# Running dV up to eight heads ahead of dK in the backward part of a decode-attention kernel

## The chip, the cores and the metric

The kernel runs on one core of one Trainium2 chip. A core has five engines with a stream of instructions each: TensorE (PE, matmuls), VectorE (DVE), ScalarE (ACT), GpSimd (POOL) and SyncE (SP). SyncE only waits and issues transfers between the chip's main memory and the on-chip memory; the transfers are carried out by 16 DMA engines. The metric is the time of one execution on the device, in microseconds (us). Before the change it is 1714.82 us, the median of three runs (1712.49 to 1715.11).

## The reference

What is computed is the forward pass of one transformer block for one new token in each of four sequences, with the attention against a cache, and then the gradients of eight of its inputs, the two caches among them:

```python
def _A_ref(x, k_cache, v_cache, wq, wo):       # B=4, Sq=1, D=512; H=32, Sk=4096, Dh=128
    q = (x @ wq).reshape(B, Sq, H, Dh).transpose(0, 2, 1, 3)
    scores = einsum("bhqd,bhkd->bhqk", q, k_cache) * Dh ** -0.5
    p = softmax(scores)
    o = einsum("bhqk,bhkd->bhqd", p, v_cache)
    return o.transpose(0, 2, 1, 3).reshape(B, Sq, H * Dh) @ wo
h  = x + _A_ref(layernorm(x), k_cache, v_cache, wq, wo)
h2 = h + swiglu(layernorm(h), w1, w3, w2)      # F=1792
# outputs: h2, and the gradients of x, k_cache, v_cache, wq, wo, w1, w3, w2 for a given grad_out
```

There are 4 x 32 = 128 pairs of sequence and head; the kernel calls each pair a head and numbers them s = 0 to 127. The K and the V of a head are 4096 x 128 numbers in bf16 each, 1024 KB. For a single query the gradients of the caches are outer products. With dO the gradient of the head's output o:

- dV = p (4096 numbers) times dO (128 numbers): it needs p and dO, and no cache.
- dP = V dO, and from it dS = p (dP - c) times the scale, with c = the sum of o dO.
- dK = dS (4096 numbers) times q (128 numbers): it needs dP, and so V once more.

## The kernel before

The program order of each engine is the order in which the code below calls its instructions. The forward part reads every K and V once. The backward part, which the change touches, reads every V a second time and writes 128 dV and 128 dK of 1024 KB each.

**Slots.** All large tiles live in 23 slots of on-chip memory. A slot that is given back is appended to a queue and taken again from its front; whoever takes it waits until the work that still uses it is over. In the backward part seven slots make up a ring of their own for V. At the beginning four are left for the outputs dV and dK; more come free later.

```python
def outer(dst, col2, row):                     # one VectorE multiply of 128 x 4096
    nc.vector.tensor_tensor(out=dst..., in0=col2..., in1=row..., op=ALU.mult)

def grad_V(s):
    gv = Slot("gv")
    outer(gv.heads(), P2s.pop(s), reps["rdo", s // REP][:, s % REP, :])
    nc.sync.dma_start(out=rows_of(out_3[b, h]), in_=gv.heads())
    if s > 1: gv.give()
    else:     first_gv.append(gv)              # dV(0) and dV(1): given back later

def grad_K(s):
    gk = Slot("gk")
    outer(gk.heads(), dS2s[s // B][:, s % B], reps["rq", s // REP][:, s % REP, :])
    nc.sync.dma_start(out=rows_of(out_2[b, h]), in_=gk.heads())
    gk.give()
```

`outer` needs the row (dO or q of the head) on all 128 partitions. `replicate` makes this for a group of REP = 4 heads: four matmuls against columns of the identity, and a ScalarE copy into one of two buffers in turn. `P_pairs` is a GpSimd copy that lays out p for `outer`, in three buffers in turn.

```python
def replicate(i0):
    for nm_, rows in (("rdo", dOrows_bf), ("rq", qrows_bf)):
        if (nm_, i0 // REP) in reps: continue
        ps = psrep.tile([P, REP, Dh], FP32, tag="rep", name="rep_ps")
        for i in range(REP): nc.tensor.matmul(ps[:, i, :], lhsT=ident_b[...], rhs=rows[0:K_, :], ...)
        rt = rep_bufs[nm_][i0 // REP % 2]
        nc.scalar.copy(out=rt, in_=ps[:])
        reps[nm_, i0 // REP] = rt
```

**The front of a head** makes its row of dP. V lies with the 4096 keys on the partitions and has to be transposed first:

```python
def front(s):
    for g in range(4):                         # V_T: 8 PE transposes, one ScalarE copy back over V
        V_T(s, psT, range(g, g + 1))
        if s % 4 == 0 and g == 0: rows_out()   # the last group's four rows of dP: PSUM to SBUF
        if s % 4 == 0 and g == 2: rows_T()     # ... and transposed on PE
    dO_window(s + 2)                           # GpSimd: the dO column for a later front
    # 8 matmuls: dP of the head into rows of one PSUM tile
    # the slot of V(s) goes to the ring (or to the outputs, when the ring has its seven)

def group_dS(g): ...                           # VectorE: dS of four heads, from the transposed dP
```

**The loop.** `load_ahead` issues a load of V for each slot in the ring. All transfers below are issued by SyncE, in this order: one whose data or slot isn't ready holds up those behind it. At most eight are in flight, as each waits for the eighth before it.

```python
# dV(0), dV(1) have been issued in the stage before
O0, S0, L, LV = 2, 21, 5, 3
for s in range(L):
    load_ahead(s); P_pairs(s); front(s)
    if s < 2:        first_gv[s].give()
    elif s < LV + 1: grad_V(s)
group_dS(0)
for s in range(NH):
    load_ahead(s + L)
    if s % REP == 0 and s + REP < NH: replicate(s + REP)
    P_pairs(s + L)
    if s + L < NH: front(s + L)
    elif s + L == NH: rows_out(); rows_T()
    if s > 0 and s + LV < NH: grad_V(s + LV)
    grad_K(s)
    if s % B == B - 1 and s + 1 < NH: group_dS((s + 1) // B)
    if s >= S0: step("s", 3 if s < S0 + 15 else 2)   # pieces of the weight gradients and of dx
    elif s >= O0: step("o")                          # pieces of dO for the later heads
```

Of the kernel before, what the change touches and what calls it, by code (L numbers as in the profile page):

```python
# [9 lines left out]
FP32 = mybir.dt.float32  # L10
# [14 lines left out]
def kernel(  # L25
# [22 lines left out]
    nc = tc.nc  # L48
    P = nc.NUM_PARTITIONS
# [5 lines left out]
    Dh = A_k_cache.shape[3]  # L55
    F = B_w1.shape[1]
    NH = B * H
# [105 lines left out]
    ident_b = const.tile([P, P], BF16, name="ident_b")  # L163
# [14 lines left out]
    def ones_window(col):  # L178
# [11 lines left out]
                          in_=rowg[:, None, :, None].to_broadcast([P, 4, 8, 4]))  # L190
# [70 lines left out]
    with ExitStack() as c0:  # L261
# [11 lines left out]
        for h in range(H):  # L273
            for cc in range(DC):
                nc.tensor.matmul(qT_ps[:, h, :], lhsT=wq_s[cc].b(HD)[:, h * Dh:(h + 1) * Dh], rhs=xhatT[:, cc, :],
                                 start=(cc == 0), stop=(cc == DC - 1))
# [4 lines left out]
        for r in range(2):  # L281
            for t_ in range(2):
                for q in range(4):
                    nc.tensor.matmul(qr_ps[32 * q:32 * (q + 1), 2 * r + t_, :], lhsT=ident_b[:, 64 * r + t_:64 * (r + 1):2],
                                     rhs=qT_bf[:], start=True, stop=True, tile_position=(0, 32 * q))
# [314 lines left out]
    def step(k, n=1):  # L600
        for _ in range(n):
            next(units[k], None)
# [114 lines left out]
    dOrows_bf = pers2.tile([NH, Dh], BF16, name="dOrows_bf")  # L717
# [4 lines left out]
    qrows_bf = pers2.tile([NH, Dh], BF16, name="qrows_bf")  # L722
# [29 lines left out]
    REP = B  # L752
    reps = {}
# [13 lines left out]
    P2s, first_gv = {}, []  # L767

    def outer(dst, col2, row):
        nc.vector.tensor_tensor(  # L770
            out=dst.rearrange("p j (r t) -> p j r t", t=2),
            in0=col2[:, :, None, :].to_broadcast([P, SJ, Dh // 2, 2]),
            in1=row.rearrange("p (r t) -> p r t", t=2)[:, None, :, :].to_broadcast([P, SJ, Dh // 2, 2]),
            op=ALU.mult,
        )

    def grad_V(s):
        b, h = bh_of(s)
# [3 lines that stand above are left out]
        if s > 1:  # L782
            gv.give()
        else:
            first_gv.append(gv)
# [14 lines left out]
    with ExitStack() as cm:  # L800
# [33 lines left out]
        for wi, wt in enumerate((w1, w3)):  # L834
            for fc in range(FC):
                for cc in range(DC):
                    nc.tensor.matmul(gu_ps[:, wi, fc, :], lhsT=w13_view(wt, cc)[:, fc * P:(fc + 1) * P], rhs=hhatT[:, cc, :],
                                     start=(cc == 0), stop=(cc == DC - 1))
# [25 lines left out]
        for jj in range(DC):  # L864
            i_mm = 0
            for (lt, wt) in ((d_gateT_bf, w1), (d_upT_bf, w3)):
                for fc in range(FC):
                    nc.tensor.matmul(dn_ps[:, jj, :], lhsT=w13_view(wt, jj)[:, fc * P:(fc + 1) * P], rhs=lt[:, fc, :],
                                     start=(i_mm == 0), stop=(i_mm == 2 * FC - 1))
                    i_mm += 1  # L870
        for sl in w1 + w3:
            sl.give()
        rs = Slot("reps")
        rep_bufs = {nm_: [rs.b()[:, (2 * k + i) * 512:(2 * k + i + 1) * 512].rearrange("p (i d) -> p i d", i=REP) for i in range(2)]
                    for k, nm_ in enumerate(("rq", "rdo"))}
# [4 lines left out]
        ps = psA.tile([P, REP, Dh], FP32, tag="rT", name="repq_ps")  # L880
# [4 lines left out]
        for s in range(3):  # L885
# [8 lines left out]
                         start=True, stop=True)  # L894
# [32 lines left out]
    with ExitStack() as c2:  # L927
        psT = c2.enter_context(tc.tile_pool(name="psT2", bufs=2, space=bass.MemoryType.PSUM))
        psD = c2.enter_context(tc.tile_pool(name="psD", bufs=1, space=bass.MemoryType.PSUM))
        psrep = c2.enter_context(tc.tile_pool(name="psrep", bufs=1, space=bass.MemoryType.PSUM))  # L930
# [174 lines left out]
        def rest_of_dO():  # L1105
            for pg in range(1, H // 8):
                while wo_units and wo_units[0] < 4 * (pg + 1):
                    woT_unit(psT, wo_units.popleft(), "s")
                    yield
                dO_columns(8 * pg, 8 * pg + 8, psg, "gps")  # L1110
                yield
                dO_rows(8 * pg, 8 * pg + 8, psg, "gps")
                mid_w["wo"][pg].give()
                yield
            dr_ps = psg.tile([B, D], FP32, tag="gps", name="dr_ps")
            for c in range(DC):
                nc.tensor.transpose(dr_ps[:, c * P:(c + 1) * P], dhT_f[:, c, :], ident_f[:])
            nc.scalar.copy(out=dh, in_=dr_ps[:])

        units["o"] = rest_of_dO()  # L1120
        def replicate(i0):
            K_ = 8 * B if i0 < 8 * B else P
            for nm_, rows in (("rdo", dOrows_bf), ("rq", qrows_bf)):
                if (nm_, i0 // REP) in reps:
                    continue
                ps = psrep.tile([P, REP, Dh], FP32, tag="rep", name="rep_ps")
                for i in range(REP):
                    nc.tensor.matmul(ps[:, i, :], lhsT=ident_b[0:K_, i0 + i:i0 + i + 1].to_broadcast([K_, P]), rhs=rows[0:K_, :],
                                     start=True, stop=True)
                rt = rep_bufs[nm_][i0 // REP % 2]  # L1130
                nc.scalar.copy(out=rt, in_=ps[:])  # L1131
                reps[nm_, i0 // REP] = rt

        rows = {}
        dS2s = {}
# [4 lines left out]
        def dO_window(s):  # L1140
            if s < NH:
                nc.gpsimd.tensor_copy(out=zd[s % B][:, 32:132:67], in_=dOT_bf[:, s:s + 1].to_broadcast([P, 2]))  # L1142

        def P_pairs(s):
            if s < NH and s not in P2s:
                P2s[s] = bw3.tile([P, SJ, 2], BF16, tag="P2", name="P2")
                nc.gpsimd.tensor_copy(out=P2s[s][:], in_=P_all[:, s, :, None].to_broadcast([P, SJ, 2]))  # L1147

        def rows_out():
            if "ps" in rows:  # L1150
                rows["sb"] = bw3.tile([P, 512], FP32, tag="dPr", name="dPr", bufs=1)
                nc.scalar.copy(out=rows["sb"][:], in_=rows.pop("ps")[:])  # L1152

        def rows_T():
            if "sb" in rows:
                sb = rows["t"] = rows.pop("sb")
                rows["T"] = psD.tile([P, B, P], FP32, tag="dPT", name="dPT_ps")
                for jj in range(4):
                    nc.tensor.transpose(rows["T"][:, jj, :], sb[:, jj * P:(jj + 1) * P], ident_f[:])  # L1159
# [46 lines left out]
                load_V2(nc.sync)  # L1206


        O0, S0, L, LV = 2, 21, 5, 3

        def load_ahead(s):
            prefetch()
            if s < NH and s not in V2s and s not in VTs:
                load_V2(nc.sync)

        for s in range(2):
            dO_window(s)
        for s in range(L):
            load_ahead(s)
            P_pairs(s)  # L1220
            front(s)
            if s < 2:
                first_gv[s].give()
            elif s < LV + 1:
                grad_V(s)
        group_dS(0)
        for s in range(NH):
            load_ahead(s + L)
            if s % REP == 0 and s + REP < NH:
                replicate(s + REP)  # L1230
            P_pairs(s + L)
            if s + L < NH:
                front(s + L)
            elif s + L == NH:
                rows_out()
                rows_T()
            if s > 0 and s + LV < NH:
                grad_V(s + LV)
            grad_K(s)
            if s % B == B - 1 and s + 1 < NH:  # L1240
                group_dS((s + 1) // B)
            if s >= S0:
                step("s", 3 if s < S0 + 15 else 2)
            elif s >= O0:
                step("o")
# [31 lines left out]
```

## Time and profile before

The profile is of one execution of 1712.58 us, with a span of 1710.6 us from its first to its last instruction.

| | busy us | share of the span |
|---|---|---|
| PE matmuls | 1253.6 | 73% |
| PE weight loads | 928.1 | 54% |
| VectorE | 1236.0 | 72% |
| ScalarE | 968.4 | 57% |
| GpSimd | 410.8 | 24% |
| transfers | 707.50 MB | mean 414 GB/s |

The shares are averages over stages: the forward part takes about the first 660 us, a short middle stage (the second layernorm, the MLP, its gradients, dO) follows to about 700 us, and the rest is the backward loop. The rows of slices cut the span into 40 equal parts of 42.8 us, and each digit is a share in tenths. In a timeline, a row has its start, its duration, the engine, the line of the kernel, the operation, what it writes and reads, and, in brackets, for how long the engine was idle before it and what ended that. L781 is the issue of a dV, L1201 that of a dK, L797 that of a load of V; `gv` and `gk` are the tiles of dV and dK. The multiplies behind dV and dK (L770) take 2.3 us each on VectorE.

### The profile page before, as it was taken

The page shows a single profiled execution, that of the slowest core. Times are in us where ns is not written, and L with a number is a line of the kernel's source. Part 1 is how long each engine was busy: PE and PEld are TensorE (multiplying, and loading weights), DVE is VectorE, ACT ScalarE, POOL GpSimd, SP SyncE. Part 2 cuts the span into 40 slices and gives each one's busy share as a digit, 9 for nine tenths or more (in the row PEclk, how much of TensorE's full clock was granted, in tenths as well). Part 3 has the DMA queues.
Part 4 walks back from the last instruction along what each step waited for, and adds up shares of the span by engine and source line. Part 5 has one row for each costly group of instructions (what it writes and reads, how often), then busy time and mean ns, then how long its engine had stood idle before and what let it go on. Part 6 is the DMA issues. An engine that isn't in the chain of part 4 may idle for free. (4 is left out here: it accounts for less than half of the span.)

```text
span 1710.6 us, 38404 instructions
## 1 busy us (share of the span) xinstructions
PE 1253.6 (73%) x16180; PEld 928.1 (54%) x16180; DVE 1236.0 (72%) x1294; ACT 968.4 (57%) x1502; POOL 410.8 (24%) x680
## 2 busy tenths in 40 slices
PE   5889888888888888776689977766566665666650
PEld 4777766767676666644467755533344433443440
DVE  5989999999998996467677457765476566566672
ACT  3556444544544444677664468775668665675540
POOL 1211232222222321132112146420022223300220
PEclk9999999999999999899886589995889787787775
DMA  9999999999999999899999999999999999999996
GB/s 401 424 425 423 425 423 425 424 424 423 416 423 411 422 407 399 311 389 426 425 425 426 426 397 425 425 426 426 426 426 426 425 424 420 424 423 413 410 424 280
DMA packets 101741, 707.50 MB, mean 414 GB/s; under 512 B 11052, under 2 KB 15288, under 8 KB 17600
## 3 DMA queue, kind: packets, MB, share of 16 engines
q1 hardware_dynamic: 101152, 704.95, 99.0%
q8 instruction: 127, 2.08, 0.5%
q14 instruction: 46, 0.38, 0.1%
q0 software_dynamic: 416, 0.10, 0.0%
HBM read 422.59 MB, written 282.34 MB: 412 GB/s over the span
## 5 line engine op out<-in xcount | busy, mean ns | idle before, releaser
L765 ACT COPY V<-pt_tps 128x1024 bf16<-128x1024 bf16 x512 | 490.2, 1025 | 146.3 <-PE pt_tps L764 124.3
L764 PE MATMUL pt_tps<-ident_b,V 128*128 128x128 bf16 x4096 | 359.1, 249 | 206.3 <-ACT V L765 178.9
L764 PEld LDWEIGHTS <-V 128*128 128x128 bf16 x4096 | 306.7, 114 | 271.1 <-issue 231.1
L770 DVE TENSOR_TENSOR gv<-P,reps 128x4096 bf16<-128x4096 bf16 x125 | 286.9, 2295 | 162.9 <-DMA out_dram<-gv 115.5
L770 DVE TENSOR_TENSOR gk<-dS,reps 128x4096 bf16<-128x4096 bf16 x128 | 293.3, 2293 | 95.3 <-DMA out_dram<-gv 85.4
L421 DVE TENSOR_TENSOR PK<-Kn,PK 128x4096 bf16<-128x4096 bf16 x128 | 292.4, 2284 | 26.1 <-POOL PK L417 25.7
L436 PE MATMUL M_ps<-PK,Vn 128*128 128x130 bf16 x4096 | 285.2, 222 | 30.9 <-DMA Vn<-in_A_v_cache_dram 30.4
L436 PEld LDWEIGHTS <-Vn 128*128 128x128 bf16 x4096 | 253.2, 99 | 50.5 <-DMA Vn<-in_A_v_cache_dram 42.0
L1147 POOL COPY P<-P_all 128x64 bf16<-128x64 bf16 x127 | 121.5, 957 | 552.7 <-DVE gv L770 547.6
L328 DVE STREAM_TRANSPOSE KT<-Kn 128x512 f32<-128x512 f32 (+1 forms) x321 | 250.7, 797 | 0.3 <-issue 0.2
L323 ACT COPY KT<-pt_tps 128x1024 bf16<-128x1024 bf16 x128 | 129.5, 1012 | 184.9 <-PE pt_tps L322 150.1
L1177 PE MATMUL dP_ps<-V,zd 128*32 128x512 bf16 x1024 | 182.9, 439 | 66.7 <-ACT V L765 64.0
L334 POOL TENSOR_TENSOR W<-qrep,wmask 128x128 bf16<-128x128 bf16 x128 | 124.0, 969 | 82.1 <-PE S_ps L354 67.4
L417 POOL COPY PK<-P_all 128x64 bf16<-128x64 bf16 x128 | 32.6, 255 | 414.3 <-ACT P_all L411 411.3
L1142 POOL COPY zd<-dOT_bf 128x2 bf16<-128x2 bf16 x128 | 116.2, 908 | 65.7 <-PE dP_ps L1177 65.7
L1177 PEld LDWEIGHTS <-zd 128*32 128x32 bf16 x1024 | 37.6, 95 | 156.3 <-issue 141.1
L1131 ACT CAST reps<-rep_ps 128x512 bf16<-128x512 f32 x62 | 36.4, 586 | 129.4 <-DVE gk L770 97.7
L1191 DVE TENSOR_SCALAR dPr<-dPT_ps,c_rep 128x32 f32<-128x32 f32 x128 | 23.2, 242 | 89.3 <-PE dPT_ps L1159 89.2
L411 ACT COPY P_all<-pt_P 32x64 bf16<-32x64 bf16 x256 | 52.1, 204 | 53.2 <-PE pt_P L407 50.9
L322 PE MATMUL pt_tps<-ident_b,Kn 128*128 128x128 bf16 x1024 | 80.5, 223 | 0.0
L446 PE MATMUL kP_ps<-PK,onesw 128*32 128x512 bf16 x1024 | 79.2, 386 | 0.0
L386 ACT ACTIVATE E<-S_ps,nm 128x256 f32<-128x256 f32 x64 | 30.4, 475 | 82.0 <-DVE nm L383 82.0
(239 smaller groups left out, 1315.0 us busy)
## 6 DMA issues: line engine op xcount, KB each, us to landing
Kn<-in_A_k_cache_dram SPq DMA_DIRECT2D x128, 1024.0 KB, 15.3
Vn<-in_A_v_cache_dram SPq DMA_DIRECT2D x128, 1024.0 KB, 15.6
V<-in_A_v_cache_dram SPq DMA_DIRECT2D x128, 1024.0 KB, 19.8
out_dram<-gv SPq DMA_DIRECT2D x128, 1024.0 KB, 20.0
out_dram<-gk SPq DMA_DIRECT2D x128, 1024.0 KB, 20.1
wq<-in_A_wq_dram SPq DMA_DIRECT2D x8, 1024.0 KB, 15.5
out_dram<-gw SPq DMA_DIRECT2D x6, 896.0 KB, 19.7
wo<-in_A_wo_dram SPq DMA_DIRECT2D x4, 1024.0 KB, 11.7
```

The lines of the kernel that those rows point to most:

```text
L322: nc.tensor.transpose(pt[:, i, :], Kn[:, c * GW + i, :], ident_b[:])
L323: nc.scalar.copy(out=KT[:, c * GW:(c + 1) * GW, :], in_=pt[:])
L328: nc.vector.transpose(out=KT[:, c * w_:(c + n) * w_], in_=Kn[:, c * w_:(c + n) * w_])
L334: nc.gpsimd.tensor_tensor(out=W[:, hl], in0=qrep[:, :, s:s + 1].to_broadcast([P, 4, 32]), in1=wmask[:, hl, None, :].to_broadcast([P, 4, 32 ...
L421: nc.vector.tensor_tensor(out=PK[:, :, 0:Dh].rearrange("p j (r t) -> p j r t", t=2), in0=Ks[s].heads().rearrange("p j (r t) -> p j r t", t=2),
L436: nc.tensor.matmul(hold["M"][:], lhsT=Vn[:, j, :], rhs=PK[:, j, :], start=(j == 0), stop=(j == SJ - 1))
L764: nc.tensor.transpose(pt[:, i, :], v[:, g * GW + i, :], ident_b[:])
L765: nc.scalar.copy(out=v[:, g * GW:(g + 1) * GW, :], in_=pt[:])
L770: nc.vector.tensor_tensor(out=dst.rearrange("p j (r t) -> p j r t", t=2), in0=col2[:, :, None, :].to_broadcast([P, SJ, Dh // 2, 2]), in1=r ...
L1142: nc.gpsimd.tensor_copy(out=zd[s % B][:, 32:132:67], in_=dOT_bf[:, s:s + 1].to_broadcast([P, 2]))
L1147: nc.gpsimd.tensor_copy(out=P2s[s][:], in_=P_all[:, s, :, None].to_broadcast([P, SJ, 2]))
L1177: nc.tensor.matmul(rows["acc"][32 * c:32 * (c + 1), :], lhsT=zq_window(zd[hl], 2 * hl + u), rhs=VT[:, j0:j0 + 4, :], start=(hl == 0 and u ...
```

## The change

dV needs neither V nor dP, only p and the replicated dO rows, so it can be made long before the dK of its head. The old loop keeps dV three heads ahead of dK. The new one lets it run further ahead from the beginning of the backward part, up to eight heads, and lets the lead fall back to three from head 60 to head 76. Three things go with it. The slots of the first two dV are both given back after the first front, instead of after the first and the second, so that the next dV can take them sooner. The replicated rows of dO and of q are made apart, each shortly before its own user. And p of heads 3 to 5 is laid out before the first front.

The aim is that the output transfers have work while the fronts of the first heads are still to come.

```diff
-        def replicate(i0):
+        def replicate(nm_, i0):
+            if i0 >= NH or (nm_, i0 // REP) in reps:
+                return
 ...                                            (the body as before, for one kind of row)
-        O0, S0, L, LV = 2, 21, 5, 3
+        O0, S0, L = 2, 21, 5
+        gvd = {"n": 2}
+
+        def more_V(upto):
+            while gvd["n"] < min(NH, upto):
+                s = gvd["n"]
+                P_pairs(s)
+                replicate("rdo", s - s % REP)
+                grad_V(s)
+                P_pairs(s + 1)
+                P_pairs(s + 2)
+                gvd["n"] += 1
+                if s % REP == 2:
+                    replicate("rdo", s + 2)
+
+        def lead_V(s):
+            return 8 - min(5, max(0, s - 56) // 4)
 ...
+        for s in range(3, 6):
+            P_pairs(s)
         for s in range(L):
             load_ahead(s)
-            P_pairs(s)
             front(s)
-            if s < 2:
-                first_gv[s].give()
-            elif s < LV + 1:
-                grad_V(s)
+            if s == 0:
+                for gv in first_gv:
+                    gv.give()
+            more_V((4, 6, 7, 8, 9)[s])
+            if s == 0:
+                replicate("rdo", REP)
         group_dS(0)
         for s in range(NH):
             load_ahead(s + L)
-            if s % REP == 0 and s + REP < NH:
-                replicate(s + REP)
-            P_pairs(s + L)
+            if s % REP == 2:
+                replicate("rq", s + 2)
 ...
-            if s > 0 and s + LV < NH:
-                grad_V(s + LV)
+            if s > 0:
+                more_V(s + 1 + lead_V(s))
             grad_K(s)
```

More of the change, by code (lines that the diff above doesn't have):

```diff
@@ L1120 @@
         units["o"] = rest_of_dO()
-        def replicate(i0):
+        def replicate(nm_, i0):
+            if i0 >= NH or (nm_, i0 // REP) in reps:
+                return
             K_ = 8 * B if i0 < 8 * B else P
[L1123 to L1132, printed above, removed]
+            rows = dOrows_bf if nm_ == "rdo" else qrows_bf
+            ps = psrep.tile([P, REP, Dh], FP32, tag="rep", name="rep_ps")
+            for i in range(REP):
+                nc.tensor.matmul(ps[:, i, :], lhsT=ident_b[0:K_, i0 + i:i0 + i + 1].to_broadcast([K_, P]), rhs=rows[0:K_, :],
+                                 start=True, stop=True)
+            rt = rep_bufs[nm_][i0 // REP % 2]
+            nc.scalar.copy(out=rt, in_=ps[:])
+            reps[nm_, i0 // REP] = rt
         rows = {}
```

## The prediction

> **What bounds the kernel now.** I read the page first (part 2, the slices), then windows of 10 us around the one slice that falls out, then the timelines of SyncE's transfers and of VectorE there, and last the waits.
>
> ```profile
> PE   5889888888888888776689977766566665666650
> ...
> PEclk9999999999999999899886589995889787787775
> DMA  9999999999999999899999999999999999999996
> GB/s 401 424 425 423 425 423 425 424 424 423 416 423 411 422 407 399 311 389 426 425 425 426 426 397 425 425 426 426 426 426 426 425 424 420 424 423 413 410 424 280
> ```
> No compute engine is full, and the transfers run at about 425 GB/s almost everywhere. The page's 707.50 MB at 425 GB/s take 1665 us, so of a span of 1710.6 us only some 46 us are lost. The slices show where: slice 17 (684 to 727 us, 311 GB/s), slice 18 (389) and the last one (280). A change of order can win only what such holes hold. This is the beginning of the backward part, by windows (the last two columns are the DMA share and GB/s):
>
> ```profile
> 700.00:710.00 10.00, 6.79 (x59) 4.42 (x56) 7.37 (x7) 5.92 (x7) 5.59 (x13) 0.66 0.89 367
> 710.00:720.00 10.00, 6.95 (x85) 4.32 (x80) 0.00 (x0) 7.52 (x8) 0.72 (x4) 1.00 0.40 107
> 720.00:730.00 10.00, 6.87 (x84) 4.66 (x80) 6.51 (x8) 7.52 (x10) 1.98 (x4) 1.00 0.88 308
> 730.00:740.00 10.00, 7.00 (x84) 4.34 (x82) 5.96 (x3) 7.53 (x9) 3.58 (x4) 1.00 0.96 331
> 740.00:750.00 10.00, 7.23 (x80) 4.36 (x78) 5.56 (x7) 7.54 (x9) 2.38 (x2) 1.00 1.01 421
> ```
> Short of 425 by 58, 318, 117 and 94 GB/s, the four windows from 700 to 740 us lose 587 x 10 / 425 = 13.8 us. In the second, VectorE is not busy at all. Its timeline and SyncE's say why:
>
> ```profile
> 707.25 2.29 DVE L770 TENSOR_TENSOR gv<-P,reps 128x4096 bf16<-128x4096 bf16 x1
> 723.31 0.73 DVE L1191 TENSOR_SCALAR dPr<-dPT_ps,c_rep 128x32 f32<-128x32 f32 x4 [13.77 <-PE dPT_ps L1159]
> ```
> ```profile
> 700.22 7.26 SPq L781 DMA_DIRECT2D out_dram<-gv  x3
> 715.45 0.34 SPq L797 DMA_DIRECT2D V<-in_A_v_cache_dram  x1
> 715.88 0.38 SPq L781 DMA_DIRECT2D out_dram<-gv  x1
> 720.44 5.87 SPq L797 DMA_DIRECT2D V<-in_A_v_cache_dram  x2
> 726.85 0.34 SPq L1201 DMA_DIRECT2D out_dram<-gk  x1
> 732.34 0.33 SPq L797 DMA_DIRECT2D V<-in_A_v_cache_dram  x1
> ```
> After four dV, VectorE waits 13.77 us for the dP of the first group of heads. Meanwhile nothing may go out: the next load of V waits until front(2) has released a slot (715.45), and the finished fourth dV stands behind it in SyncE's order. A front takes some 5 us (PE transposes, four ScalarE copies of 1025 ns, dP matmuls) and releases one load.
>
> [...]the shortest landing of a dV in the hole is 4.3 us, and 1024 KB at 425 GB/s are 2.47 us, which leaves 1.8. So one transfer at a time does not fill the engines, and it takes two or more in flight. [...]dV work, which needs no dP, goes into the stretch that waits for fronts. [...]the P copies here take 0.23 us beside an idle VectorE and 2.34 us beside a dV.
>
> **The change part by part.** *Amount of work.* None is added or removed: the same 128 dV (2.29 us each), 128 dK, as many replications (four matmuls and one ScalarE copy of 586 ns), the same bytes. Only order and slots change.
>
> *The opening.* Slots: the outputs still take turns in the same four, and the loads in the ring of seven. In the program's order seven dV transfers now precede the first ring load; then load, dV, load, dV, load, dK. Worked from the old times: dV(0) to dV(2) are unmoved (issued 700.2, 702.8, 707.1), since dV(2) takes V(0)'s slot after front(0). dV(3) may go out at once, at 709.6. dV(4) needs dV(1)'s slot (landed by about 707), the second group of replicated rows (matmuls and copy after front(0), some 1 us, in time) and its P: VectorE 709.5 to 711.8. dV(5) takes dV(2)'s slot, landed at 707.1 + 4.3 = 711.4: done 714.1. dV(6) takes dV(3)'s: 716.4. dV(7) takes V(1)'s, free since front(1): 718.7. dV(8) takes dV(4)'s: 721.0. So from 707 on one transfer goes out every 2.3 us, against 2.47 us that each takes, and from 716 on the loads come on top. The two replications put into the opening delay fronts 2 to 4 by about 1 us, and dK(0) from 726.8 to 727.7. Then front(5) no longer has two replications ahead of it and ends at about 732, as before.
>
> *The sum.* At 733.3 us the old order has issued dV 0 to 4, dK 0 and 1 and four loads since 700. The new one has issued dV 0 to 9, the same two dK and four loads: five transfers more at the same head of the fronts and of dK. 5 x 2.47 = **12.3 us**. That fits the 13.8 us that the hole holds: about 1.5 us stay (start of the first transfers, 706 to 709).
>
> *Where it is cashed.* The lead itself does not shorten the middle: at the same time the same head is in front and dK, with five more dV away. It is spent at heads 60 to 76, where five iterations leave out a dV. In the old trace dK(60) goes out at 1191 us and dK(76) at 1316, and there
>
> ```profile
> 1190.00:1320.00 130.00, 77.78 (x780) 48.30 (x780) 80.42 (x56) 83.65 (x105) 21.66 (x35) 0.85 1.01 426
> ```
> the transfers are full and PE, VectorE and ScalarE are busy 60%, 62% and 64%. Taking 12.3 us out of 130 brings PE to 66% and ScalarE to 71%. I take the whole gain as cashed. From head 76 on the lead is three again and the end is as before: the 20 us from 1690 on, at 127 GB/s, lose 14 us in both kernels.
>
> *Replicated rows made apart.* In the old order the replicated q rows for head s+4 are made at head s, into a buffer that dK(s-1) still reads, so ScalarE, and with it the next front, waits for VectorE:
>
> ```profile
> ACT reps L1131 <- DVE gk L770: 97.7, 18, 12.5
> ```
> Now they are made at head s+2 of the group before, into a buffer last read by dK five heads back from the new ones: fronts may run two heads further ahead. Off the path mostly, as the transfers are full. It helps where PE is the slower one: from 960 to 1000 us it is busy 87% at a granted clock of 0.61, SyncE waits for fronts, and just after it the transfers sink to 364, 401 and 388 GB/s (990 to 1020), a loss of 61 + 24 + 37 = 122, or 2.9 us. A larger lead of the fronts should fill part; I count 1 us.
>
> Together 12.3 + 1.0 = 13.3 us: 1714.8 - 13.3 = **1701.5 us**.
>
> **The rivals.** (a) *The gain is given back at the fronts.* Heads 60 to 76 must pass 12 us faster; if PE, slowed by its clock, can't, part is lost. For it: granted clocks of 0.5 in some windows from 1150 on. Against it: SyncE's waits from 1110 to 1400 us are for landed transfers nearly all, for PE 2.5 us. It would give 1705 to 1712. (b) *SyncE's order turns on the new kernel.* A dV now stands ahead of the next load; if a dV is late for its slot, the load behind it is late too, and later a front. For it: four output slots only, and in the old trace from 745 to 860 us SyncE waits 36.5 us for dV and 29.3 for dK. Against it: these waits lie under full transfers. It would give about 1708 to 1718. (c) *The slack of the fronts does more than I count*, and the dip at 990 to 1020 and the 401 to 413 GB/s from 1550 to 1620 us go too: 2 to 4 us more, 1697 to 1699. Slower by 2% would need a new hole of 34 us, and faster by 2% a time of 1680.5, which is the 1665 us of bytes plus the unchanged end: there is no room.
>
> **Range and chances.** Three runs of before spread over 2.6 us. Around 1701.5 I put 1696 (rival c with all of the hole) to 1709 (half of the gain given back). Chances: faster by over 2% 0.01, within 2% 0.97, slower by over 2% 0.02.
>
> **What would show it.** Right: the windows from 710 to 740 us at 400 GB/s or more, VectorE busy from 707 to 721; dK(0) issued at 727 to 728 and dK of the same head at nearly the same time until 60; five heads' transfers caught up by head 76; a span 11 to 14 us shorter. Wrong: low GB/s that returns within 710 to 800 us, fronts that start later than before, or GB/s under 420 from 1190 to 1320, where the lead is spent.

## The result, and the profile after

The changed kernel takes 1703.23 us, the median of four runs (1702.52 to 1705.36); the kernel before took 1714.96 us beside it, also in four. The ratio is 0.9937, with a 95% interval of 0.9920 to 0.9954. The prediction was 1701.5 us in a range of 1696 to 1709. The profiled spans are 1710.6 us before and 1700.7 us after, 9.9 us apart.

The slices of the kernel after (40 of 42.5 us; each digit a share in tenths, the last row the GB/s moved):

```profile
PE   5889888888888888877689877676577666666660
...
PEclk9999999999999999899976789988787877777665
DMA  9999999999999999999999999999999999999996
GB/s 401 424 425 423 424 424 424 423 424 424 414 424 411 422 406 401 385 419 425 425 425 426 425 424 425 425 426 426 424 422 422 419 421 415 419 421 410 412 425 280
```

Two things are to be seen. Slice 17, which stood at 311 GB/s, is now at 385. And in slices 30 to 36 the rate is lower than before, 422 to 415 where it had been 426 to 420. Nobody had planned for the second.

The same stretch by windows of 10 us, and the stretch in which the lead is spent (PE, PE weight loads, VectorE, ScalarE, GpSimd busy; granted clock; DMA share; GB/s):

```profile
700.00:710.00 10.00, 6.97 (x65) 4.89 (x63) 7.96 (x8) 5.76 (x8) 3.38 (x13) 0.66 0.86 356
710.00:720.00 10.00, 6.95 (x84) 4.46 (x83) 9.58 (x5) 7.72 (x9) 7.74 (x7) 1.00 1.01 418
720.00:730.00 10.00, 7.00 (x79) 4.38 (x77) 6.66 (x8) 7.49 (x10) 4.44 (x5) 1.00 0.99 361
730.00:740.00 10.00, 7.15 (x84) 4.39 (x82) 5.09 (x4) 7.76 (x10) 1.35 (x5) 1.00 1.00 423
...
1190.00:1320.00 130.00, 87.12 (x812) 55.06 (x811) 74.41 (x58) 86.96 (x110) 24.05 (x36) 0.83 1.01 423
```

Against 425 GB/s the four windows of the hole now lack 69 + 7 + 64 + 2 = 142, or 142 x 10 / 425 = 3.3 us, where they lacked 13.8. So 10.5 us of bytes were won here. PE is as busy as it was in the second to fourth window; what changed is VectorE, from 0.00 to 9.58 us in the second. SyncE's issues (start, duration, line, what is written and read, count) and VectorE's operations show the five transfers themselves:

```profile
700.74 16.61 SPq L781 DMA_DIRECT2D out_dram<-gv  x7
717.46 0.78 SPq L797 DMA_DIRECT2D V<-in_A_v_cache_dram  x1
719.22 0.33 SPq L781 DMA_DIRECT2D out_dram<-gv  x1
721.81 0.34 SPq L797 DMA_DIRECT2D V<-in_A_v_cache_dram  x1
722.25 0.53 SPq L781 DMA_DIRECT2D out_dram<-gv  x1
727.34 0.34 SPq L797 DMA_DIRECT2D V<-in_A_v_cache_dram  x1
728.24 0.33 SPq L1201 DMA_DIRECT2D out_dram<-gk  x1
732.33 0.34 SPq L797 DMA_DIRECT2D V<-in_A_v_cache_dram  x1
732.76 0.45 SPq L781 DMA_DIRECT2D out_dram<-gv  x1
733.31 0.44 SPq L1201 DMA_DIRECT2D out_dram<-gk  x1
```
```profile
707.56 6.72 DVE L770 TENSOR_TENSOR gv<-P,reps 128x4096 bf16<-128x4096 bf16 x3
714.70 6.73 DVE L770 TENSOR_TENSOR gv<-P,reps 128x4096 bf16<-128x4096 bf16 x3 [0.42 <-POOL P L1147]
724.70 0.73 DVE L1191 TENSOR_SCALAR dPr<-dPT_ps,c_rep 128x32 f32<-128x32 f32 x4 [3.27 <-PE dPT_ps L1159]
```

Up to 733.3 us ten dV (7 + 1 + 1 + 1), two dK and four loads have been issued; before it were five dV, two dK and four loads. The last dV and dK of the old count are these:

```profile
732.76 0.38 SPq L781 DMA_DIRECT2D out_dram<-gv  x1
733.23 0.38 SPq L1201 DMA_DIRECT2D out_dram<-gk  x1
```

VectorE's wait for the first dP is 3.27 us in place of 13.77. Of what is left of the hole, nearly half lies in the first window, which lacked as much before (356 GB/s now, 367 then), and nearly half in the third, at 361 GB/s: behind the dV of 722.25 nothing is issued until the load at 727.34, which waits for a front (the loads' waits for dP are up to 4.5 us here).

Where the time went is clearest in the moments at which dK of the same head is issued (my list, from the issues of L1201):

| head of dK | before, us | after, us | difference |
|---|---|---|---|
| 0 | 726.8 | 728.2 | +1.4 |
| 32 | 963.7 | 965.7 | +2.0 |
| 48 | 1090.6 | 1092.7 | +2.1 |
| 64 | 1223.0 | 1220.1 | -2.9 |
| 80 | 1351.6 | 1341.3 | -10.2 |
| 112 | 1612.5 | 1602.5 | -10.0 |
| 127 | 1689.9 | 1680.0 | -9.9 |

The five dV taken out of heads 60 to 76 bring 12.1 us (from about +2.0 to -10.1), and hardly anything of that is lost afterwards.

### The profile page after: what moved, and what is told of

It is laid out like the page before. It is cut to its first block, busy times and chain, and to the rows that moved or that the text cites. A ratio compares the mean times of both kernels' runs of the same rounds, so it can differ in the third digit from the quotient of the medians.

```text
span 1700.7 us, 38400 instructions
## 1 busy us (share of the span) xinstructions
PE 1258.0 (74%) x16180; PEld 931.3 (55%) x16180; DVE 1236.7 (73%) x1294; ACT 967.2 (57%) x1502; POOL 397.8 (23%) x678
## 3 DMA queue, kind: packets, MB, share of 16 engines
q8 instruction: 127, 2.08, 0.5%
## 5 line engine op out<-in xcount | busy, mean ns | idle before, releaser
L770 DVE TENSOR_TENSOR gv<-P,reps 128x4096 bf16<-128x4096 bf16 x125 | 286.1, 2292 | 172.1 <-DMA out_dram<-gv 132.8
L770 DVE TENSOR_TENSOR gk<-dS,reps 128x4096 bf16<-128x4096 bf16 x128 | 293.4, 2294 | 111.1 <-DMA out_dram<-gv 77.3
L1177 PE MATMUL dP_ps<-V,zd 128*32 128x512 bf16 x1024 | 179.1, 432 | 68.6 <-ACT V L765 65.8
L1147 POOL COPY P<-P_all 128x64 bf16<-128x64 bf16 x125 | 92.4, 740 | 468.7 <-DVE gv L770 468.6
L1142 POOL COPY zd<-dOT_bf 128x2 bf16<-128x2 bf16 x128 | 130.5, 1021 | 156.3 <-PE dP_ps L1177 156.3
L322 PEld LDWEIGHTS <-Kn 128*128 128x128 bf16 x1024 | 62.0, 100 | 25.8 <-issue 25.8
L400 ACT ACTIVATE Pn<-E,rl 128x1024 bf16<-128x1024 f32 x64 | 73.7, 1152 | 3.3 <-DVE rl L397 3.2
```

Source lines behind the costliest of these rows:

```text
L322: nc.tensor.transpose(pt[:, i, :], Kn[:, c * GW + i, :], ident_b[:])
L770: nc.vector.tensor_tensor(out=dst.rearrange("p j (r t) -> p j r t", t=2), in0=col2[:, :, None, :].to_broadcast([P, SJ, Dh // 2, 2]), in1=r ...
L1177: nc.tensor.matmul(rows["acc"][32 * c:32 * (c + 1), :], lhsT=zq_window(zd[hl], 2 * hl + u), rhs=VT[:, j0:j0 + 4, :], start=(hl == 0 and u ...
```

## The experiments

Every kernel below is an edit of the changed kernel, if nothing else is said, and its time is a median; ratios are to the kernel before, timed beside it (medians 1712.88 to 1714.14 us).

### 1. The replicated rows coupled again

```diff
-            if s % REP == 2:
-                replicate("rq", s + 2)
+            if s % REP == 0:
+                replicate("rq", s + REP)
```

> The changed kernel, but the replicated q rows are made again at the first head of the group before (four heads ahead, into a buffer that the dK just before still reads); the lead of dV is kept. Theory A (one of the 16 DMA engines is behind the others and sets the time; a dip of the mean rate in which that engine has work left costs nothing): the dip of GB/s between 980 and 1020 us comes back, and the time stays within 1 us of the changed kernel's 1703.2 us. Theory B (bytes per time count, as the prediction had it): the dip costs 2 to 3 us, 1705 to 1706.

Measured: 1702.73 us, ratio 0.9934 (0.9919 to 0.9949). The time is that of the changed kernel, so making the rows apart is worth nothing. But the dip at 990 to 1020 us did not come back: the four windows from 980 on moved 423, 426, 423 and 426 GB/s. That part of the expectation failed: with the larger lead of dV the dip stays away even if the rows are coupled.

### 2. Only the rows apart, in the kernel before

```diff
-            if s % REP == 0 and s + REP < NH:
-                replicate(s + REP)
+            if s % REP == 0 and s + REP < NH:
+                replicate(s + REP, "rdo")
+            if s % REP == 2 and s + 2 < NH:
+                replicate(s + 2, "rq")
```

> The kernel before, with only the replicated rows of q made two heads later (apart from those of dO), lead three as before. Theory A: the dip at 980 to 1020 us is filled, the hole at 704 to 738 us stays, and the time stays within 1 us of before, 1715. Theory B: 1712 to 1713.

Measured: 1713.47 us, ratio 0.9996 (0.9988 to 1.0005): no difference. By windows of this kernel (columns as above):

```profile
710.00:720.00 10.00, 7.16 (x83) 4.32 (x80) 0.36 (x1) 7.49 (x9) 0.72 (x4) 0.98 0.35 120
720.00:730.00 10.00, 7.00 (x86) 4.75 (x84) 5.69 (x8) 7.72 (x10) 1.27 (x3) 1.00 0.90 315
...
990.00:1000.00 10.00, 7.17 (x87) 4.64 (x87) 10.00 (x6) 8.00 (x10) 10.00 (x8) 1.00 1.01 420
1000.00:1010.00 10.00, 6.83 (x92) 5.14 (x90) 6.61 (x6) 9.68 (x12) 6.63 (x6) 1.00 1.02 428
1010.00:1020.00 10.00, 7.91 (x110) 5.67 (x108) 9.97 (x8) 6.17 (x8) 6.95 (x4) 1.00 1.01 421
```

The hole is there as before, and the dip (364, 401 and 388 GB/s before) is gone, with a granted clock of 0.66 in the window ahead of it where before had 0.54. So in the old order the coupled rows do make the dip. And yet the time is the same. A dip in the rate that can be filled for nothing was not on the path. This asked for another explanation of what sets the end; it is taken up in experiments 8 to 12.

### 3. The lead at five heads, and 4. at eleven

```diff
 def lead_V(s):
-    return 8 - min(5, max(0, s - 56) // 4)
+    return 5 - min(2, max(0, s - 56) // 4)        # 3
+    return 11 - min(8, max(0, s - 56) // 4)       # 4
 ...
-            more_V((4, 6, 7, 8, 9)[s])
+            more_V((4, 5, 6, 6, 6)[s])            # 3
+            more_V((4, 6, 8, 10, 12)[s])          # 4
```

Kernel 4 also replicates rows of heads 32 to 63 from 64 rows in place of 128, since the later rows aren't made yet when it wants them.

> The changed kernel with a lead of five instead of eight (dV up to head 5 in the opening, the lead falls to three at heads 60 to 64). If the gain is the number of dV issued more by the same head of dK, times 2.47 us: two transfers instead of five, 4.9 us less 1 to 2 us for later fronts, 1710 to 1712. If the order of the opening alone does it (both slots given back after the first front, the fourth dV not behind a load), most of the gain is there already: 1703 to 1705.

> The changed kernel with a lead of eleven (dV up to head 11 in the opening, the lead falls to three at heads 60 to 88). Three transfers more would be 7.4 us if the hole went on, 1696. But the changed kernel's hole has only some 3 us left (356 GB/s at 700 to 710 us, 361 at 720 to 730), part of it before the first dV can go, so I expect 1701 to 1704: two or three us at most, against a dK(0) that goes out later.

Measured: lead five 1708.81 us, ratio 0.9966 (0.9955 to 0.9978), 5.1 us sooner than before. That is the two transfers by which its lead exceeds the old one, 2 x 2.47 = 4.9. The hole stays half open:

```profile
710.00:720.00 10.00, 6.99 (x80) 4.33 (x80) 3.91 (x2) 7.49 (x9) 4.46 (x5) 1.00 1.01 393
720.00:730.00 10.00, 7.40 (x84) 4.75 (x84) 6.25 (x8) 7.49 (x10) 3.29 (x3) 1.00 0.70 238
730.00:740.00 10.00, 6.52 (x78) 4.18 (x77) 6.13 (x3) 7.29 (x9) 3.18 (x4) 1.00 0.99 349
```

Lead eleven: 1703.09 us, ratio 0.9935 (0.9921 to 0.9950), the same as lead eight. It sends eight dV more than before ahead of dK(0), but dK(0) goes out at 735.5 us, 8.6 us later than before, and dK(48) 10.5 us later; of the eight transfers' 19.8 us so much is paid at once that 8.9 us are left at the end. With eight heads of lead the hole is full, and more transfers only push others away.

### 5. The lead spent at heads 28 to 44, and 6. never

```diff
-            return 8 - min(5, max(0, s - 56) // 4)
+            return 8 - min(5, max(0, s - 24) // 4)        # 5
+            return 8                                      # 6
```

> The changed kernel with the lead let down from eight to three at heads 28 to 44 (about 930 to 1060 us) instead of 60 to 76. There PE was busiest in the profile of before (87% at a granted clock of 0.61 from 960 to 1000 us). If the gain can be cashed wherever eight transfers are in flight, the time stays at 1702 to 1705. If the fronts set the pace there, they can't pass 12 us faster, and part of the gain is lost: 1706 to 1712.

> The changed kernel with a lead of eight to the end. The last eight heads then have no dV, only dK, and no loads of V from head 116 on: one transfer of 2.47 us per front of about 5 us. With seven fronts in hand and eight transfers in flight some of it is covered; I expect 4 to 8 us lost, 1706 to 1712. If the gain needs no place to be spent, because only the number of transfers counts: 1703.

Measured: 1703.88 us (ratio 0.9939, 0.9922 to 0.9956) and 1703.16 us (0.9937, 0.9922 to 0.9952). Kernel 5 spends where PE is slowest, and these are its windows there:

```profile
920.00:940.00 20.00, 17.67 (x136) 13.44 (x132) 13.72 (x7) 8.51 (x9) 5.87 (x6) 0.66 1.01 426
940.00:960.00 20.00, 18.53 (x132) 15.29 (x131) 6.35 (x9) 9.37 (x11) 1.91 (x4) 0.57 1.01 426
960.00:980.00 20.00, 18.04 (x155) 14.91 (x156) 12.74 (x6) 10.43 (x12) 6.36 (x5) 0.69 1.01 426
```

PE is busy 88% to 93% at clocks of 0.57 to 0.69, and the rate is still 426: rival (a) falls even at the worst place. Kernel 6, for which I had expected a loss, lost nothing. There dK runs 12.8 us behind the changed kernel from head 80 to head 112, and since all dV are then gone, the last heads send only dK and are level at the end (+0.4 us at head 126). The place where a lead is spent is free; what counts is the number of transfers that left early.

### 7. The first two slots given back as before

```diff
-            if s == 0:
-                for gv in first_gv:
-                    gv.give()
+            if s < 2:
+                first_gv[s].give()
```

> The changed kernel with the slots of the first two dV given back as before, the first after front 0 and the second after front 1. dV(4) then takes the slot of dV(2) (landed about 711.5 us) instead of that of dV(1) (about 707), and dV(5) that of dV(3): each some 2.4 us later, while two transfers are still in flight. 1703 to 1705: 0 to 2 us of the gain hang on it.

Measured: 1705.27 us, ratio 0.9949 (0.9934 to 0.9964). Giving the two slots back together brings about 2 us (kernels 5 and 6, timed beside it, took 1703.88 and 1703.16).

### 8. No transposes of V from head 60 on

```diff
-        for g in part:
+        for g in part if s < 60 else ():
```

This leaves out the 32 transposes and the four ScalarE copies of each of these heads, so their dK is made from V that is not transposed; all transfers stay. It asks whether what makes one DMA engine end late hangs on PE's instructions.

> The changed kernel without the 32 PE transposes and 4 ScalarE copies of V in the fronts of heads 60 to 127: it leaves work out, so dK of these heads and what comes of it are not the reference's. The bytes of loads and outputs are the same. In the profile one DMA engine ends some 12 us after the others. If it is late through fetching PE's instructions (4352 fewer here), it falls behind less from 1190 us on and the end comes 3 to 10 us earlier, 1693 to 1700. If its delay has nothing to do with PE, and the transfers are full anyway, the time stays within 1 us of 1703.

Measured: 1694.60 us, ratio 0.9889 (0.9875 to 0.9904), 8.6 us below the changed kernel. It is not that fronts held up the transfers and no longer do. These are SyncE's longest waits in this kernel from 1200 to 1660 us (what waits, for what: us in total, times, the longest), and then those of the changed kernel:

```profile
SPq L1201 <- DMA V<-in_A_v_cache_dram: 62.4, 31, 2.6
SPq L797 <- DMA out_dram<-gk: 62.4, 30, 2.2
```
```profile
SPq L797 <- DMA out_dram<-gk: 64.7, 30, 2.3
SPq L1201 <- DMA V<-in_A_v_cache_dram: 61.8, 31, 2.7
```

Both wait for transfers to land, as long and as often. So why did the transposes matter? PE runs 4352 instructions less (2176 matmuls and as many weight loads), and the page's queue q8, of the kind "instruction", has 110 packets in place of 127.

### 9. The same number of PE instructions, without their work

In place of the 32 transposes, 32 matmuls over four columns; no ScalarE copies. The dK of these heads is again left undone.

```diff
+        for g in part if s >= 60 else ():
+            pf = ps.tile([P, GW, 4], FP32, tag="tps", name="pt_few")
+            for i in range(GW):
+                nc.tensor.matmul(pf[:, i, :], lhsT=v[:, g * GW + i, :], rhs=ident_b[:, 0:4], ...)
```

> As x8 (the ScalarE copies of V of heads 60 to 127 left out, outputs that hang on them not the reference's), but each of the 32 transposes is replaced by a matmul over 4 columns with the same weights, so PE runs as many instructions as the changed kernel in less time. If x8 was faster because fewer instructions are fetched, the time goes back to that of the changed kernel, 1702 to 1704. If it was faster because the fronts were relieved, it stays at 1694 to 1697.

Measured: 1705.61 us, ratio 0.9957 (0.9943 to 0.9972), with 127 packets on q8. The gain of kernel 8 is gone, although the copies and two thirds of the transposes' time on PE are still left out (PE is busy 77.1 of the 180 us from 1320 to 1500, against 118.3 in the changed kernel and 58.6 in kernel 8). (It is 2.4 us above the changed kernel, which has as many packets; why, I can't say.)

### 10. Every tenth dK sent as two transfers

Twelve dK in all are sent as 120 rows and 8 rows. It asks whether the end moves when the rows are shared out to the engines in another way.

```diff
+            if s % 10 == 9:
+                nc.sync.dma_start(out=rows_of(out_2[b, h])[0:120], in_=gk.heads()[0:120])
+                nc.sync.dma_start(out=rows_of(out_2[b, h])[120:P], in_=gk.heads()[120:P])
```

> The changed kernel with every tenth dK (heads 9, 19, ... 119, twelve in all) sent as two transfers, of 120 and of 8 rows, all outputs as the reference's. [...]If the engine that ends last is the sixteenth, the lone end at some 28 GB/s goes and the time falls to 1690 to 1697; if it is one of the first eight, the time rises by 2 to 5 us; if it is another, it stays at 1703 within 1.5.

Measured: 1722.16 us, ratio 1.0060 (1.0043 to 1.0076). The trace has 84 packets of 4 B more, and doesn't name their engines; a whole transfer has 16 of them, and 12 x (15 + 8 - 16) is 84, which agrees with 15 and 8 engines for the two parts. The numbers of the engines in the expectation were my assumption; the runs don't show them. What this run shows is a price: each split costs about 1.3 us of span ((1716.1 - 1700.7) / 12), or 1.6 between the medians. That it is because a split takes two of the eight places in flight was not tested. The end still looks like that of one lone engine, with 16 to 31 GB/s for 10 us up to 1714 us (next section). If 120 rows leave out one engine, and if that were the late one, 12 x 64 KB less should have freed it, which speaks against it; but the splits upset so much that I call this inconclusive.

### 11. V transposed as pairs: a kernel that computes everything

If PE's instructions cost time as such, then V should be transposed with fewer of them. A block of 128 x 128 32-bit numbers holds two blocks of bf16: 16 transposes per head in place of 32.

```diff
-        v = VTs[s].heads()
+        v = VTs[s].b().bitcast(FP32).rearrange("p (n x) -> p n x", x=P)
         for g in part:
-            pt = ps.tile([P, GW, P], BF16, tag="tps", name="pt_tps")
-            for i in range(GW):
-                nc.tensor.transpose(pt[:, i, :], v[:, g * GW + i, :], ident_b[:])
-            nc.scalar.copy(out=v[:, g * GW:(g + 1) * GW, :], in_=pt[:])
+            pt = ps.tile([P, GW // 2, P], FP32, tag="tps", name="pt_tps")
+            for i in range(GW // 2):
+                nc.tensor.transpose(pt[:, i, :], v[:, g * GW // 2 + i, :], ident_f[:])
+            nc.scalar.copy(out=v[:, g * GW // 2:(g + 1) * GW // 2, :], in_=pt[:])
 ...                                       # in front(): moving V of even, then of odd columns
-            VT = VTs[s].heads()
+            VT = VTs[s].b().rearrange("p (n x t) -> p n x t", x=P, t=2)
-                    ... lhsT=zq_window(zd[hl], 2 * hl + u), rhs=VT[:, j0:j0 + 4, :] ...
+                    ... lhsT=zd[hl][:, a:a + 32],           rhs=VT[:, 4 * c:4 * c + 4, :, u] ...
```

After such a transpose, partitions 0 to 63 hold the pairs of an even key and 64 to 127 those of an odd one. So the stationary of dP has dO of even (or odd) columns in one column for the upper half and in the next for the lower half; two small GpSimd copies per head fill it, from dO columns split by eight matmuls per page. `group_dS` reads the rows in the order that follows. Nothing is left out.

> The changed kernel, with V transposed as 32-bit pairs: 16 transposes of 128x128 fp32 in place of 32 of bf16 per head, nothing of the computation left out. PE runs 128 x 16 x 2 = 4096 instructions fewer (a weight load and a matmul each) and 128 more for the dO columns split by even and odd, so about 15 or 16 packets of instructions fewer than 127. Theory[...]: the same bytes end some 8 us sooner, as where the transposes were left out from head 60 on (17 packets, 8.6 us): 1695, range 1693 to 1698. Rival (only the work taken from the fronts counts, and here PE and ScalarE keep most of it): no more than 2 us sooner than the changed kernel, 1701 to 1704. Second rival: the fp32 transposes and the copies of fp32 are slower than those of bf16 and hold up the fronts: 1705 or more, with waits for PE in SyncE.

Measured: 1697.50 us (five runs, 1696.87 to 1699.59), ratio 0.9907 (0.9893 to 0.9921): 5.7 us faster than the changed kernel. The page's engine line, the instruction queue and the three rows of this front (line, engine, operation, what is written and read, count, busy us and mean ns, idle before):

```profile
PE 1249.1 (74%) x14164; PEld 913.3 (54%) x14164; DVE 1239.5 (73%) x1298; ACT 768.7 (45%) x1502; POOL 456.1 (27%) x806
...
q8 instruction: 112, 1.84, 0.4%
...
L772 PE MATMUL pt_tps<-ident_f,V 128*128 128x128 f32 x2048 | 381.9, 347 | 130.4 <-DMA V<-in_A_v_cache_dram 103.7
L773 ACT COPY V<-pt_tps 128x512 f32<-128x512 f32 x512 | 290.5, 589 | 346.0 <-PE pt_tps L772 340.8
```

PE is as long busy as before (1258.0 us there), for one transpose takes 347 ns in place of 250. ScalarE is 198 us less busy, which experiment 9 showed to be worth nothing. What fell is the count: 2016 matmuls and as many weight loads, and 15 packets. From head 16 on the head-by-head list agrees with a price per instruction and not with a gain at one place: dK, 2.9 us sooner at head 0 but 0.2 later at head 16, is 0.6 us sooner at head 32, 1.6 at 48, 2.5 at 64, 3.2 at 80, 5.0 at 112 and 5.5 at 127.

### 12. The instructions doubled

As kernel 9, but each of the 32 matmuls over four columns is made twice (the second time into the same columns again).

```diff
-            for i in range(GW):
-                nc.tensor.matmul(pf[:, i, :], lhsT=v[:, g * GW + i, :], ...)
+            for i in range(2 * GW):
+                nc.tensor.matmul(pf[:, i % GW, :], lhsT=v[:, g * GW + i % GW, :], ...)
```

> The dose of instructions doubled. As in the kernel with 32 matmuls over 4 columns per head in place of the 32 transposes (from head 60 on), but with 64 such matmuls; the transposes and the ScalarE copies are left out, so the gradients of K of these heads are not computed. The transfers are the same bytes. PE then runs 64 x 2 instructions per head there, against 0 and 32 x 2 in the two kernels before. Theory[...]: 17 packets of instructions more, about 144, and the end another 9 to 11 us later: 1705.6 + 10 = 1715, range 1712 to 1719. Rival (the time follows what PE or the fronts do, and these small matmuls still leave PE with less to do than the transposes did): 1703 to 1708.

Measured: 1714.95 us, ratio 1.0006 (1.0000 to 1.0013). Together with 8 and 9 this is a row of three doses, for the same transfers. One window of each of 8, 9 and 12 (columns as above):

```profile
1320.00:1500.00 180.00, 58.58 (x297) 16.13 (x297) 111.27 (x72) 30.93 (x60) 53.92 (x48) 0.50 1.01 425
```
```profile
1320.00:1500.00 180.00, 77.14 (x997) 36.26 (x996) 110.19 (x71) 31.45 (x62) 45.86 (x46) 0.50 1.01 415
```
```profile
1320.00:1500.00 180.00, 94.05 (x1692) 53.72 (x1692) 106.41 (x70) 31.18 (x61) 39.53 (x44) 0.50 1.01 408
```

| PE matmuls per head from 60 on, in place of 32 transposes | packets on q8 | time, us | span, us |
|---|---|---|---|
| 0 (kernel 8) | 110 | 1694.60 | 1694.5 |
| 32 small (9) | 127 | 1705.61 | 1703.3 |
| 64 small (12) | 144 | 1714.95 | 1712.6 |

PE is busy for a third to a half of the window in all three, ScalarE for a sixth; neither can be the bound. Each dose is 4352 instructions of PE (and 17 packets) more and takes 8.8 and 9.3 us of span; between the medians it is 11.0 and 9.3, as the profiled execution of kernel 8 was the slowest of its four. That is 2.0 to 2.5 ns an instruction.

In these three kernels the instructions and PE's reads of V (by the trace, each of these weight loads reads a block of 128 x 128) grow together. Kernel 11 parts them: there V is read once as before, with 12% fewer instructions of PE in all, and the time falls. That speaks for the count.

## What sets the end

The tail holds the key. I had written that the last 20 us lose 14 us in both kernels, and left it there. This is the end of the changed kernel in steps of 0.53 us (from 1680 us to 1701):

```profile
DMA  9999999877421000000000000000000000000000
GB/s 437 421 437 406 437 453 390 343 297 296 172 125 78 31 31 31 31 16 31 31 16 31 31 16 31 31 31 16 31 31 16 31 31 31 16 31 0 0 0 0
```

From the 14th step on, 12 us long, 16 to 31 GB/s are moved. By an estimate from the mean rate, one of 16 engines has 425 / 16 = 26.6 GB/s. The 39 packets of 8192 B that start after 1687 us follow each other at 0.306 us and take 0.309, one at a time, which is 26.8. So I read the end as one engine that works off a backlog while 15 have finished.

How long it has been behind can be read from the signals of landing. Each transfer gives 16; the trace holds their times, but not their engines. That each stands for one engine's part is my reading: the last transfer's 16th signal comes 11.8 us after its 15th in the changed kernel, and the lone packets take as long. This is how long after the 15th signal of a transfer the 16th comes (medians of the transfers that land in each stretch, my list):

```
us                300-500  740-800  900-1000  1100-1200  1300-1400  1500-1600  last transfer
kernel before         0.1      1.0       3.6        4.7        8.1       12.0           12.1
changed kernel        0.1      0.1       3.0        7.0       10.7       12.4           11.8
kernel 11             0.2      0.2       2.2        5.6        8.3       11.9           11.6
```

So one part of each transfer falls behind in the backward part and stays some 12 us late, five parts of 64 KB at 2.45 us (eight packets at 0.306). What comes next waits for this part. In both traces no transfer of SyncE is issued before the 16th signal of the eighth before it, and from 1200 to 1660 us half of them are issued within 64 ns after it. VectorE waits for slots until transfers of dV have landed, 132.8 us ahead of the dV multiplies and 77.3 ahead of those of dK in the changed kernel. So in the end the late engine sets the pace: in the changed kernel the last signals follow each other at 2.51 us from 1200 to 1660 us, and the mean rate of 417 GB/s from 1240 to 1600 us is one transfer of 1024 KB in 2.51 us. That it is always the same engine is inferred from the steady growth of the lag. The spacing also shows why the dip of the old kernel was free: from 990 to 1020 us, with the mean at 364 to 401 GB/s, the last signals came every 2.53 us, as from 940 to 990 (2.50).

Why is it late? The spacing of the last signals from 1200 to 1660 us follows the doses: 2.474 us in kernel 8, 2.522 in 9 and 2.568 in 12, and about 2.45 in each after 1660 us, when PE is all but done. Some 200 transfers go out from head 60 to the end, so a step of 0.048 or 0.046 us makes 9.6 or 9.2 us: the price of a dose. And the long spacings lie where PE's small matmuls do. In kernel 12 the 57 spacings with 30 matmuls or more average 2.78 us, the other 121 2.47; in kernel 9 it is 2.68 (57) and 2.45 (124).

I had taken the packets that bring PE's instructions for the cause. The page of the changed kernel lists 127 packets on q8 with 2.08 MB (16384 B each in the trace). Their number goes with PE's instructions: 17 packets for each 4352 in kernels 8, 9 and 12 are 256 instructions to a packet, and 2 x 16180 over 256 are 126.4. But the signals speak against these packets being on the late engine. Each takes 0.98 us in the trace, and by my estimate an engine that has no time to spare would show it. In the changed kernel the last signals are 2.516 us apart where such a packet falls between them (21 times) and 2.510 where none does; in kernel 12 2.540 (34 times) and 2.574. It is the 15th signals that come later there, 2.71 us apart for 2.46 (changed kernel, 1100 to 1660 us). And in the forward part, with 11 of these packets in 100 us against 4 to 7 in the backward part, nothing lags (0.1 us from 300 to 500 us).

So the late part of each transfer and its dependence on the number of PE's instructions are shown, and the way from the one to the other is open. The lag shows in the backward part alone, and nothing in the signals points to q8.

## Why the prediction was right, and where it wasn't

- *The five transfers.* Right: exactly five more by 733.3 us, dV(3) to dV(8) issued within 1.3 us of the forecast moments (the last, dV(8), at 722.25 for 721.0), and 12.1 us cashed at heads 60 to 76, for 12.3 predicted. Kernel 3 repeats the sum with two transfers (5.1 for 4.9).
- *What stays of the hole.* I wrote about 1.5 us; 3.3 us stay. The difference, 1.8 us, is near the term that is missing in the sum: dK of the same head runs 1.4 us later at head 0 and 2.0 at head 32, where I had it "at nearly the same time". Of dK(0)'s 1.4 us I had predicted 0.9. dV(0) itself went out 0.5 us later in this run (700.74 for 700.22); why was not looked into.
- *Replicated rows apart, 1 us.* The mis-sized term: kernels 1 and 2 show no gain within their noise (0.5 us). The step that failed is "a larger lead of the fronts should fill part" of the dip, counted as bytes won. The dip does fill; but the late engine had a backlog of 3.6 us and did not dip, so nothing was won. By bytes the changed kernel was 13.1 us ahead after the dip (10.3 before it), and gave the difference back between 1240 and 1600 us, at 417 GB/s for 422.
- *The unchanged end.* Right as a number, and not understood: I took the mean of 425 GB/s for the bound. It is unchanged because the lag of the late engine had stopped growing at about 12 us in both kernels, which I did not know.
- *Rival (a)*, the gain lost at the fronts: falls with kernel 5. *Rival (b)*, SyncE's order: the 2.0 us by which heads run later may be its small core, and there is no more. *Rival (c)*, more from slack: falls with kernels 1 and 2. ("401 to 413 GB/s from 1550 to 1620 us" left out one window of 422.)
- *The markers.* Three came out short: 361 GB/s from 720 to 730 us where I asked for 400, dK(0) at 728.2 for 727 to 728, and a span 9.9 us shorter for 11 to 14. My marker "GB/s under 420 from 1190 to 1320" would not have told anything: it stood at 423 there, and fell to 415 later without harm.

The sum is then 12.1 - 2.0 = 10.1 us, against 9.9 between the spans and 11.7 between the medians (the kernel before had medians of 1712.88 to 1714.96 us in its six sets of runs, so 10 to 12 is as near as it can be told). The 13.3 us of the prediction were too many by the two terms above, 2.0 for the later heads and 1 for the rows.

## What to carry to other kernels

Where transfers are full except for one hole, count the transfers that the new order gets out before the hole's end, and multiply by one transfer's time (here 5 x 2.47 = 12.3 us, and 12.1 were measured); where they are missing later did not matter here (kernels 5 and 6: 1703.88 and 1703.16 us). But a mean rate near its plateau doesn't say which engine is the bound: look at the last microseconds. Here they ran at 16 to 31 GB/s, about a sixteenth of the rate, one DMA engine was behind by the signals, and the dip of the old kernel to 364 GB/s was free, as that engine had a backlog of 3.6 us. In this kernel the number of TensorE instructions cost time even where TensorE was idle for half of the time (9.3 us for 4352 from kernel 9 to 12), so one wider instruction in place of two is worth trying though it takes longer by itself (347 ns for 250 in kernel 11, which was 5.7 us faster).

## What the runs showed of the hardware that was not expected

- The number of PE's instructions cost time where the transfers were the bound: 8.8 to 11.0 us for 4352 of them, 9.3 for the next 4352, and 5.5 us of span for the 4032 fewer of kernel 11; what makes that less stays open. It is the part of each transfer that ends last that got slower, 2.78 us for 64 KB where PE ran 30 small matmuls or more, against 2.47 (kernel 12). Where a packet of q8 fell between two such ends they were no further apart (2.516 us for 2.510 in the changed kernel).
- By the signals and the rate of the end, one of 16 DMA engines fell 12 us behind the other 15 (11.8 in the changed kernel, 12.1 before) and set the end, with the mean rate at 417 to 426 GB/s.
- Transposing pairs of bf16 as 32-bit numbers took 347 ns for 128 x 128, against 2 x 250 for the two bf16 blocks, and the ScalarE copy out of PSUM 589 ns for 128 x 512 of 32 bits, against 1025 for the 128 x 1024 of 16 bits that it replaces.
- Splitting a transfer of 1024 KB into 120 and 8 rows cost 1.3 to 1.6 us where eight were in flight.
